# Attention and expert routing on one core: low parts on GpSimd, gating's count in spare columns of an output tile, rows stored in five pieces, a new order

## The chip, the core and the metric

One core of one Trainium2 chip. The metric is device time of one execution in microseconds; lower is better. The engines: PE is TensorE (matmuls; PEld its weight loads), DVE VectorE, ACT ScalarE, POOL GpSimd, SP SyncE, which here issues most of the DMAs. The clock of TensorE is granted by a throttle and can fall to half.

## The reference

```python
# q, k, v: (8 batches, 8 heads, 576, 64)
scores = scale * np.matmul(rotate(q), rotate(k).transpose(0, 1, 3, 2))   # rotate: rotary position
scores = scores - np.max(scores, axis=-1, keepdims=True)
attn = np.exp(scores)
attn = attn / (np.sum(attn, axis=-1, keepdims=True) + 1e-09)
x = np.matmul(attn, v)            # then to (4608 tokens, 512)
...
logits = x @ w_gate               # 8 experts
expert_idx = np.argmax(logits, axis=1)
gate_w = softmax(logits)[np.arange(N), expert_idx]
for e in range(8):
    mask = expert_idx == e
    out[mask] = gate_w[mask, None] * (np.maximum(x[mask] @ w1[e], 0) @ w2[e])   # 512 -> 1024 -> 512
```

## The kernel before

**Stages.** The first 610 us or so are attention, pair by pair: 8 batches of 4 pairs of heads (NP = 4), 32 pairs. Once a batch's four pairs are done, its rows are *gated*: logits (they come out of the matmul of O with the gate's weights beside the rows), maximum, softmax, one-hot of the chosen expert, a count (how many earlier rows chose the same expert) and a rank; the rows are stored to HBM (`x_dram`) and each row's number is written by an indirect DMA to its place in the expert's list (`xlist`). Then the experts' work runs over those lists, in slots of rows gathered by index; TensorE is busy through that stage, and the change does not touch it.

**Precision.** Scores are computed in two parts: a number is split into a high part (a copy rounded to fp32r) and a low part (the number less its high part), and three products high-high, low-high, high-low are summed.

**The order.** `PLAN` is a list of 67 tokens that `window(w)` goes through once for every w; a token ("S1p", 1) does step S1 of pair n = w - 1, and its last letter names the engine (p PE, v DVE, a ACT, g POOL, d a DMA issued on SP). So several pairs are in flight. Instructions of PE, DVE, ACT and POOL are chained in this order on their own engine. `GATE` places the steps of gating between the tokens: position `pos` means token pos % 67 of the window that lies pos // 67 after the last pair of the batch. `paced` makes a DMA wait for the last ACT instruction that was put into the order ahead of it.

**The steps of one pair.** FQ, FK load q and k (576 KB each: a copy and its rotated partner), VP loads v. RQ, RK rotate them: three 576-element operations on POOL each (`rotate`, L374 to L378), into one buffer `yq`, `yk` each. HQ, HK copy to the high part, LQ, LK subtract for the low part (L127 through `tt`, on DVE). DH, DL copy the halves of the high and of the low part to the other 64 partitions by DMA (`do_D`, L416, two DMAs each): the *moved halves*. cR gathers the last 64 columns into `zq` (L420); S4 uses that. S0 to S8 are score steps on PE (12 matmuls for S4 and 6 for each other one); M their row maximum (DVE, L444), E the exponential (ACT, L455). Scores lie in two PSUM banks of `ps_s`; O takes one of the same two. TA, TB, TR transpose; cA, cB, c1, c2, c3 copy the transposed weights to SBUF (L393). V0 to V9 multiply with v (L513); U copies the result; O transposes it back and adds the logits' columns (L534), X0 and X1 scale it into the batch's rows, ZD and RZ handle the row sums.

**Gating.** gL, gM, gD, gQ, gF, gB, gO, gV (DVE) lead from logits to the one-hot `oh`; gE, gG, gW give the weight; gP is the count on PE (`counted_`, matmuls at L645 and L647) in a bank of `ps_s` of its own; gR the rank from it (DVE); gU, gY the place; gS the store on SP (L624, L625: 1152 KB and 144 KB); gI0 to gI4 the indirect DMAs (L666, on POOL, paced). Inside the count:

```python
pc = bank()                                  # before: a tile of ps_s
nc.tensor.matmul(pc[:, 0:40], lhsT=upb, ...)
...
nc.tensor.matmul(pc[:, 64:72], lhsT=onesb, ...)
```

Of the kernel before, what the change touches and what calls it, by code (L numbers as in the profile page):

```python
# [7 lines left out]
F32 = mybir.dt.float32  # L8
# [26 lines left out]
]  # L35
GATE = [
    ("gLv", 246), ("gMv", 250), ("gDv", 250), ("gQv", 250), ("gFv", 250), ("gBv", 250), ("gOv", 250), ("gVv", 250),
    ("gEa", 252), ("gGv", 260), ("gWv", 260), ("gPp", 261), ("gSd", 265), ("gRv", 275), ("gUv", 283), ("gYv", 283),
    ("gI0g", 300), ("gI1g", 300), ("gI2g", 334), ("gI3g", 334), ("gI4g", 367),
]  # L40
W0 = -2
WARM = 80
RSTEP = (15, 17, 18, 45, 49, 50, 58)
WSPLIT = (24, 30, 47, 62)
NR = 2
CHAINED = ("EngineType.PE", "EngineType.DVE", "EngineType.Activation", "EngineType.Pool")


# [13 lines left out]
def kernel(  # L62
# [21 lines left out]
    cpool = ctx.enter_context(tc.tile_pool(name="cpool", bufs=1))  # L84
# [18 lines left out]
    x_dram = dpool.tile([NT, H * XW], F32, name="x_dram")  # L103
# [6 lines left out]
    V = nc.vector  # L110
    sm = ctx.enter_context(tc.tile_pool(name="sm", bufs=3))
# [14 lines left out]
    def tt(o, x, y, op):  # L126
        V.tensor_tensor(out=o, in0=x, in1=y, op=op)  # L127
# [270 lines left out]

    def do_LQ(st, n, eng):
        q = st["q"]  # L400
        tt(q[:, 0, 1], st["yq"], q[:, 0, 0].bitcast(F32), ALU.subtract)

    def do_HK(st, n, eng):
        st["k"] = rp.tile([P, 2, 2, HS], F32R, name="k2")
# [2 lines left out]
    def do_LK(st, n, eng):  # L407
        k = st["k"]
        hi, lo = (k[:, i].rearrange("p h s -> p (h s)") for i in range(2))
        tt(lo, st["yk"], hi.bitcast(F32), ALU.subtract)  # L410

    def do_D(st, n, part):

# [114 lines left out]
    def do_O(st, n):  # L528
# [24 lines left out]
    def do_X(st, n, h):  # L553
        b, pr = divmod(n, NP)
        nc.vector.tensor_tensor(
            out=batch(b)[:, :, 2 * pr + h, :], in0=st["O"][:, h, 0:5 * XW].rearrange("p (c w) -> p c w", w=XW),
            in1=st["rz"][:, :, h:h + 1].broadcast_to([P, 5, XW]), op=ALU.mult)

    def perform(tok, st, n):

# [19 lines left out]
        else:  # L580
            dict(RQ=do_RQ, RK=do_RK, ZD=do_ZD, RZ=do_RZ, O=do_O, TR=do_TR, cR=do_cR)[name](st, n)

    def gate(b, bank, spaced=True):

        batches.pop(b)
        xt = xt2[b % 2]
        L = sm.tile([P, 5, E], F32, name="L")
        mx = sm.tile([P, 5], F32, name="mx")
        dl = sm.tile([P, 5, E], F32, name="dl")
        ex, rk = gate_ex, gate_rk  # L590
        gs = sm.tile([P, 5], F32, name="gs")
# [16 lines left out]
        def at(eng):  # L608
            return nc.gpsimd if eng == "g" else V
# [10 lines left out]
        def weight(eng):  # L620
            V.reciprocal(out=xt[:, :, 0], in_=gs)

        def store(eng):
            nc.sync.dma_start(out=x_dram[b * S:b * S + 512, :].rearrange("(p i) d -> p i d", i=4), in_=xt[:, 0:4])  # L624
            nc.sync.dma_start(out=x_dram[b * S + 512:b * S + 576, :], in_=xt[0:64, 4])  # L625

        def equal(eng):
            tt(eq, L, mxb, ALU.is_equal)

        def scored(eng):  # L630
            at(eng).tensor_tensor(out=eq, in0=eq, in1=C("escore").unsqueeze(1).broadcast_to([P, 5, E]), op=ALU.mult)

        def best(eng):
            V.tensor_reduce(out=bs, in_=eq, axis=AX.X, op=ALU.max)

        def onehot(eng):
            tt(eq, eq, bs.unsqueeze(2).broadcast_to([P, 5, E]), ALU.is_equal)

        def masked(eng):
            at(eng).tensor_tensor(out=oh, in0=eq, in1=C("valid").unsqueeze(2).broadcast_to([P, 5, E]), op=ALU.mult)  # L640

        def counted_(eng):
            pc = bank()
            count.append(pc)
            nc.tensor.matmul(pc[:, 0:40], lhsT=upb, rhs=oh.rearrange("p c e -> p (c e)"), start=True, stop=False)  # L645
            for c in range(4):
                nc.tensor.matmul(pc[:, 8 * c + 8:40].rearrange("p (c e) -> p c e", e=E), lhsT=onesb,  # L647
                                 rhs=oh[:, c:c + 1, :].broadcast_to([P, 4 - c, E]), start=False, stop=(c == 3))
            for c in range(5):
                nc.tensor.matmul(pc[:, 64:72], lhsT=onesb, rhs=oh[:, c], start=(c == 0), stop=(c == 4))  # L650
# [13 lines left out]
        def listed(c):  # L664
            def f(eng):
                ins = nc.gpsimd.indirect_dma_start(  # L666
                    out=xlist, out_offset=bass.IndirectOffsetOnAxis(ap=lpi[:, c:c + 1], axis=0),
                    in_=tid[:, 5 * b + c:5 * b + c + 1], in_offset=None,
                    bounds_check=E * LCAP - 1, oob_is_err=False)
                tc.declare_no_dep(ins.ins, group="xlist", reason="the entries are disjoint")  # L670
                tc.add_to_no_dep_group("xlist", ins.ins)
                scattered.append(ins.ins)
                if spaced:
                    paced(ins)
            return f

        return dict(gL=logits, gM=top, gD=below, gE=exps, gG=total, gW=weight, gS=store, gQ=equal, gB=best,
                    gF=scored, gO=onehot, gV=masked, gP=counted_, gR=rank, gU=own, gY=place,
                    **{f"gI{c}": listed(c) for c in range(5)})

    def first_slots():
        assert len(scattered) == 5 * (B - 2)
# [37 lines left out]

    def gate_step(tok, b, ordered):
        if b not in gates:
            gates[b] = gate(b, lambda: ps_s.tile([P, 2, 512], F32, name="sp")[:, 0])
        chained_emit(lambda: gates[b][tok[:-1]](tok[-1]), ordered)

    def window(w, more={}, keep=lambda tok, n: True):
# [31 lines left out]
    def setup():  # L758

        nc.vector.tensor_copy(out=upb, in_=C("upper"))  # L760
        nc.vector.tensor_copy(out=tid, in_=C("tid"))
        nc.vector.tensor_copy(out=run, in_=C("ebase"))
        nc.vector.tensor_copy(out=gate_rk[:, :, E:E + 1], in_=C("bad").unsqueeze(2))
        for a, g in ((0, 0), (64, D)):
            r = slice(a, a + 64)
            nc.vector.tensor_copy(out=iw[r, :, E - g // 8:E - g // 8 + D], in_=ident[r, r].unsqueeze(1).broadcast_to([64, NP, D]))
            nc.sync.dma_start(out=iw[r, :, g:g + E], in_=w_gate.rearrange("(r p) e -> p r e", r=NP)[r])
        nc.sync.dma_start(out=xlist.rearrange("(p c) o -> p (c o)", p=P), in_=mark)
# [241 lines left out]
    reload(1, 2, regs1)  # L1010
    xtrans(1, 2)
    mm2(0, hs0, 2, False)
    last = gate(B - 1, lambda: ps_y.tile([P, DM], F32, name="yp"), False)
    for name, _ in GATE:
        last[name[:-1]](name[-1])
    slot(1, 2)
    route_rest()
    nc.gpsimd.memset(xsm, 0.0)
# [112 lines left out]
```

## Time and profile before

| | us |
|---|---|
| three runs, median (lowest to highest) | 1125.07 (1121.01 to 1126.71) |
| the profiled execution, its span | 1127.2, 1125.4 |
| TensorE busy in the span | 1027.6 (91%) |
| DVE, ACT, POOL busy | 737.2, 655.6, 417.6 |
| mean granted clock of TensorE | 0.940 of full speed |

A time at the head of a row is the start in the span; square brackets behind a row of the timeline hold how long the engine stood idle before it and on what, for example `<-DMA qk`. Rows of a group give the total busy time and the mean in ns of one. A share of the span averages stages: attention and the experts' stage have to be read apart, and attention window by window.

### The profile page before, as it was taken

The page shows a single profiled execution, that of the slowest core. Times are in us where ns is not written, and L with a number is a line of the kernel's source. Part 1 is how long each engine was busy: PE and PEld are TensorE (multiplying, and loading weights), DVE is VectorE, ACT ScalarE, POOL GpSimd, SP SyncE. Part 2 cuts the span into 40 slices and gives each one's busy share as a digit, 9 for nine tenths or more (in the row PEclk, how much of TensorE's full clock was granted, in tenths as well). Part 3 has the DMA queues.
Part 4 walks back from the last instruction along what each step waited for, and adds up shares of the span by engine and source line. Part 5 has one row for each costly group of instructions (what it writes and reads, how often), then busy time and mean ns, then how long its engine had stood idle before and what let it go on. Part 6 is the DMA issues. An engine that isn't in the chain of part 4 may idle for free. (4 is left out here: it accounts for less than half of the span.)

```text
span 1125.4 us, 25298 instructions
## 1 busy us (share of the span) xinstructions
PE 1027.6 (91%) x9720; PEld 812.9 (72%) x9720; DVE 737.2 (65%) x1188; ACT 655.6 (58%) x1180; POOL 417.6 (37%) x329
## 2 busy tenths in 40 slices
PE   4899889998898898798978989999999999999997
PEld 4666556666565565555656778999999999998886
DVE  6777757666567576575764565656666566665897
ACT  2787657666575575565667433545555445544886
POOL 5555365554554454645525231123112221112010
PEclk6799989989898899899998989999999999999999
DMA  7444674765746747556655041674262341124992
GB/s 237 129 132 132 140 126 138 135 119 153 97 126 132 103 131 143 106 164 107 119 170 118 15 88 33 198 251 153 67 190 59 123 148 50 42 65 151 355 350 91
DMA packets 91746, 151.47 MB, mean 135 GB/s; under 512 B 23207, under 2 KB 56231, under 8 KB 90592
## 3 DMA queue, kind: packets, MB, share of 16 engines
q1 hardware_dynamic: 83328, 127.66, 45.7%
q0 software_dynamic: 8000, 20.92, 6.0%
q8 instruction: 79, 1.29, 0.5%
q10 hardware_dynamic: 288, 1.18, 0.3%
q14 instruction: 51, 0.42, 0.1%
HBM read 162.47 MB, written 21.27 MB: 163 GB/s over the span
## 5 line engine op out<-in xcount | busy, mean ns | idle before, releaser
L444 DVE TENSOR_REDUCE negm<-sp 128x1 f32<-128x576 f32 x288 | 216.1, 754 | 173.4 <-PE sp L441 157.5
L455 ACT ACTIVATE pn<-sp,negm 128x576 f32<-128x576 f32 x256 | 189.8, 742 | 120.3 <-DVE negm L444 104.9
L441 PEld LDWEIGHTS sp<-k,q 64*128 64x128 f32 x1536 | 120.4, 200 | 97.9 <-issue 42.1
L441 PE MATMUL sp<-k,q 64*128 64x288 f32 x1536 | 180.2, 343 | 10.7 <-ACT pn L455 8.9
L513 PE MATMUL tp<-PT,vn 128*64 128x288 f32 x1024 | 172.2, 436 | 5.9 <-ACT PT L393 5.9
L896 PE MATMUL hp<-xh,w1h 128*128 128x256 f32 x544 | 155.5, 286 | 3.3 <-DVE hl L865 3.3
L896 PE MATMUL hp<-xl,w1h 128*128 128x256 f32 x544 | 155.2, 285 | 0.2 <-issue 0.2
L896 PE MATMUL hp<-xh,w1l 128*128 128x256 f32 x544 | 154.9, 285 | 0.0
L393 ACT COPY PT<-tp 128x1024 f32<-128x1024 f32 (+1 forms) x128 | 113.4, 905 | 45.2 <-PE tp L473 32.3
L835 DVE TENSOR_TENSOR w2l<-r,w2h 128x1024 fp32r<-128x1024 f32 x90 | 109.3, 1232 | 36.8 <-ACT w2h L834 34.4
L928 PE MATMUL yp<-w2h,hh 128*128 128x512 f32 x320 | 127.4, 398 | 0.0
L928 PE MATMUL yp<-w2l,hh 128*128 128x512 f32 x320 | 125.2, 391 | 0.0
L928 PE MATMUL yp<-w2h,hl 128*128 128x512 f32 x320 | 125.2, 391 | 0.0
L938 POOL DMA_INDIRECT out_dram<-y,gi x34 | 34.5, 1013 | 220.0 <-DVE y L131 196.2
L835 DVE TENSOR_TENSOR w1l<-r,w1h 128x1024 fp32r<-128x1024 f32 x92 | 109.3, 1229 | 4.3 <-ACT w1h L834 3.1
L896 PEld LDWEIGHTS hp<-xh,w1h 128*128 128x128 f32 x544 | 105.3, 194 | 5.6 <-DVE hl L865 3.6
L376 POOL TENSOR_TENSOR yq<-qk,rotq 128x576 f32<-128x576 f32 x31 | 44.7, 1442 | 168.3 <-DVE q L127 82.5
L896 PEld LDWEIGHTS hp<-xl,w1h 128*128 128x128 f32 x544 | 105.3, 194 | 0.9 <-issue 0.9
L896 PEld LDWEIGHTS hp<-xh,w1l 128*128 128x128 f32 x544 | 105.4, 194 | 0.8 <-issue 0.2
L473 PEld LDWEIGHTS tp<-cst,pn 64*128 64x128 f32 x2048 | 85.5, 154 | 19.8 <-ACT pn L455 8.8
L473 PE MATMUL tp<-cst,pn 64*128 64x64 f32 x2048 | 94.2, 242 | 4.4 <-issue 2.4
L864 ACT ACTIVATE hh<-hp 128x512 fp32r<-128x512 f32 x68 | 40.7, 598 | 96.7 <-PE hp L896 90.7
(201 smaller groups left out, 1818.7 us busy)
## 6 DMA issues: line engine op xcount, KB each, us to landing
r<-in_moe_w_dram SPq DMA_DIRECT2D x192, 512.0 KB
qk<-in_qk_dram SPq DMA_DIRECT2D x64, 576.0 KB
q<-q SPq DMA_DIRECT2D x128, 144.0 KB
x_dram<-xt SPq DMA_DIRECT2D x8, 1152.0 KB
vn<-in_v_dram SPq DMA_DIRECT2D x32, 256.0 KB
x_dram<-xt SPq DMA_DIRECT2D x8, 144.0 KB
vr<-in_v_dram SPq DMA_DIRECT2D x64, 16.0 KB
xlist<-tid,lpi POOLq DMA_INDIRECT x40
```

The source lines that it names most:

```text
L376: e.tensor_tensor(out=y, in0=x[0], in1=cos, op=ALU.mult)
L393: (nc.scalar.copy if eng == "a" else nc.vector.tensor_copy)(out=o, in_=i)
L441: nc.tensor.matmul(sp[:, u, 0:HS], lhsT=lhs, rhs=st["k"][r, kp, hc], start=(i_ == 0), stop=(i_ == len(todo) - 1))
L444: nc.vector.tensor_reduce(out=st["negm"][:, j:j + 1], in_=st["S", j][:, :, 0:HS], axis=AX.XY, op=ALU.max, negate=True)
L455: nc.scalar.activation(out=pt.rearrange("p (a b) -> p a b", a=2), in_=st.pop(("S", j))[:, :, 0:HS], func=AF.Exp, bias=st["negm"][:, j:j + ...
L473: nc.tensor.transpose(tp[:, b, c:c + 64], pn[r, i, k:k + P], ident[r, r])
L513: nc.tensor.matmul(st["av"][r, half, 0:HS], lhsT=st["vn"][:, h, kt, :] if kt < 4 else vr[n % NVR][:, r], rhs=st["PT"][:, h, kt, hs] if kt ...
L835: nc.vector.tensor_tensor(out=lo, in0=src, in1=hi.bitcast(F32), op=ALU.subtract)
L864: nc.scalar.activation(out=hh, in_=hp, func=AF.Relu)
L896: m = nc.tensor.matmul(hp[:, fi], lhsT=w[:, dc, fs], rhs=x[:, dc], start=(i == 0), stop=(i == len(prods) - 1))
L928: m = nc.tensor.matmul(yp[t], lhsT=h[:, fi, ts_], rhs=w[:, fi], start=(g == 0 and fi == 0 and i == 0), stop=(g == FQ - 1 and fi == 1 and i ...
L938: sc = nc.gpsimd.indirect_dma_start(out=out, out_offset=bass.IndirectOffsetOnAxis(ap=si[:, t:t + 1], axis=0), in_=y, in_offset=None, bound ...
```

## The change

- LQ and LK run on GpSimd in place of VectorE; HQ and HK on ScalarE in place of VectorE; U and c1 on VectorE in place of ScalarE.
- The order is new: all 67 tokens stand elsewhere, and the offsets are one less, so the windows begin one earlier (W0). The loads FK, FQ, VP stand at positions 27, 42 and 48 (before: 0, 37, 1); DL at 7 and DH at 61 (before 64 and 56); cR at 37 and S4 at 38; RK 2, LQ 3, LK 29, RQ 54 on POOL; S0 to S9 and V0 to V9 are grouped in another way.
- Gating's count gP is no longer a step of GATE. It is written in `do_O` of the first pair of the next batch (CP = 0), into columns 424 to 496 of O's own tile, and the rank gR is done right behind that pair's second X.
- The store has five pieces, gS0 to gS4 (four of 32 partitions, 288 KB each, and one of 144 KB), each paced and at a place of its own; the five indirect DMAs stand at (window 4: positions 3, 29, 54) and (window 5: positions 3 and 4); before, two at window 4 position 32, two at window 4 position 66, one at window 5 position 32.
- gF and gV are gone: equality and score are one operation, and a column of constants (`gate_eq`) keeps rows beyond the batch out of the one-hot.
- The last batch's gating does count and rank behind its gO.

```diff
 PLAN = [
-    ("FKd", -1), ("VPd", 0), ("E0a", 1), ("S1p", 1), ("V5p", 3), ("S3p", 1), ("c2a", 2), ("RZv", 3), ("M1v", 1),
-    ("E1a", 1), ("V6p", 3), ("M3v", 1), ("V7p", 3), ("S7p", 1), ("V8p", 3), ("HKv", 0), ("E3a", 1), ("M7v", 1),
-    ("LKv", 0), ("S8p", 1), ("V9p", 3), ("M8v", 1), ("c1a", 2), ("cRa", 0), ("E7a", 1), ("TA0p", 1), ("S4p", 0),
-    ("M4v", 0), ("Ua", 3), ("TA1p", 1), ("E8a", 1), ("Op", 3), ("RQg", -1), ("cA0a", 1), ("E4a", 0), ("TB1p", 1),
-    ("cA1v", 1), ("FQd", -2), ("cB1a", 1), ("TB0p", 1), ("S6p", 0), ("TRp", 1), ("c3v", 3), ("X1v", 3), ("X0v", 3),
-    ("M6v", 0), ("cB0a", 1), ("E6a", 0), ("S2p", 0), ("M2v", 0), ("HQv", -1), ("E2a", 0), ("V0p", 2), ("ZDd", 2),
-    ("V1p", 2), ("S5p", 0), ("DHd", -1), ("V2p", 2), ("LQv", -1), ("M5v", 0), ("S0p", 0), ("V3p", 2), ("E5a", 0),
-    ("V4p", 2), ("DLd", -1), ("M0v", 0), ("RKg", -1),
+    ("E0a", 0), ("c2a", 1), ("RKg", -1), ("LQg", -1), ("S2p", 0), ("V5p", 2), ("V6p", 2), ("DLd", -1), ("V7p", 2),
+    ("M2v", 0), ("E6a", 0), ("E2a", 0), ("RZv", 2), ("S5p", 0), ("S8p", 0), ("V8p", 2), ("V9p", 2), ("TA0p", 0),
+    ("HKa", -1), ("M5v", 0), ("E5a", 0), ("S7p", 0), ("M8v", 0), ("Uv", 2), ("TA1p", 0), ("E8a", 0), ("M7v", 0),
+    ("FKd", -2), ("cA0a", 0), ("LKg", -1), ("Op", 2), ("cA1v", 0), ("E7a", 0), ("TB0p", 0), ("TB1p", 0), ("X0v", 2),
+    ("X1v", 2), ("cRa", -1), ("S4p", -1), ("c3v", 2), ("cB0a", 0), ("cB1a", 0), ("FQd", -3), ("S3p", -1), ("TRp", 0),
+    ("V0p", 1), ("M4v", -1), ("V1p", 1), ("VPd", -2), ("M3v", -1), ("E4a", -1), ("S1p", -1), ("E3a", -1), ("M1v", -1),
+    ("RQg", -2), ("S0p", -1), ("V2p", 1), ("V3p", 1), ("HQa", -2), ("V4p", 1), ("E1a", -1), ("DHd", -2), ("ZDd", 0),
+    ("M0v", -1), ("c1v", 0), ("S6p", -1), ("M6v", -1),
 ]
 GATE = [
-    ("gLv", 246), ("gMv", 250), ("gDv", 250), ("gQv", 250), ("gFv", 250), ("gBv", 250), ("gOv", 250), ("gVv", 250),
-    ("gEa", 252), ("gGv", 260), ("gWv", 260), ("gPp", 261), ("gSd", 265), ("gRv", 275), ("gUv", 283), ("gYv", 283),
-    ("gI0g", 300), ("gI1g", 300), ("gI2g", 334), ("gI3g", 334), ("gI4g", 367),
+    ("gLv", 180), ("gMv", 210), ("gDv", 210), ("gQv", 210), ("gBv", 210), ("gOv", 210), ("gEa", 219), ("gGv", 223),
+    ("gWv", 223), ("gS0d", 228), ("gUv", 247), ("gYv", 247), ("gS1d", 249), ("gI0g", 271), ("gS2d", 295),
+    ("gI1g", 297), ("gS3d", 316), ("gI2g", 322), ("gI3g", 337), ("gI4g", 338), ("gS4d", 362),
 ]
-W0 = -2
+W0 = -3
...
+CP = 0
...
-        tt(q[:, 0, 1], st["yq"], q[:, 0, 0].bitcast(F32), ALU.subtract)
+        (nc.gpsimd if eng == "g" else nc.vector).tensor_tensor(out=q[:, 0, 1], in0=st["yq"], in1=q[:, 0, 0].bitcast(F32), op=ALU.subtract)
...
-        tt(lo, st["yk"], hi.bitcast(F32), ALU.subtract)
+        (nc.gpsimd if eng == "g" else nc.vector).tensor_tensor(out=lo, in0=st["yk"], in1=hi.bitcast(F32), op=ALU.subtract)
...
+        if n >= NP and n % NP == CP:
+            gates[n // NP - 1]["gP"](o[:, 0, 424:496])        # end of do_O
...
+        st["X"] = st.get("X", 0) + 1                           # end of do_X
+        if st["X"] == 2 and n >= NP and pr == CP:
+            gates[b - 1]["gR"]("v")
...
-        def store(eng):
-            nc.sync.dma_start(out=x_dram[b * S:b * S + 512, :].rearrange("(p i) d -> p i d", i=4), in_=xt[:, 0:4])
-            nc.sync.dma_start(out=x_dram[b * S + 512:b * S + 576, :], in_=xt[0:64, 4])
+        def store(g):
+            def f(eng):
+                if g < 4:
+                    r = slice(32 * g, 32 * g + 32)
+                    o, i = x_dram[b * S:b * S + 512, :].rearrange("(p i) d -> p i d", i=4)[r], xt[r, 0:4]
+                else:
+                    o, i = x_dram[b * S + 512:b * S + 576, :], xt[0:64, 4]
+                ins = nc.sync.dma_start(out=o, in_=i)
+                if spaced:
+                    paced(ins)
+            return f
...
-            tt(eq, L, mxb, ALU.is_equal)
-            at(eng).tensor_tensor(out=eq, in0=eq, in1=C("escore")..., op=ALU.mult)
+            V.scalar_tensor_tensor(out=eq[:, :, 0:E], in0=dl, scalar=0.0,
+                                   in1=C("escore")..., op0=ALU.is_equal, op1=ALU.mult)
...
-            pc = bank()
+        def counted_(pc):
             count.append(pc)
```

More of the change, by code (lines that the diff above doesn't have):

```diff
@@ L26 @@
 PLAN = [
[8 rows of a table removed]
[8 rows of a table added]
 ]
 GATE = [
-    ("gLv", 246), ("gMv", 250), ("gDv", 250), ("gQv", 250), ("gFv", 250), ("gBv", 250), ("gOv", 250), ("gVv", 250),
-    ("gEa", 252), ("gGv", 260), ("gWv", 260), ("gPp", 261), ("gSd", 265), ("gRv", 275), ("gUv", 283), ("gYv", 283),
-    ("gI0g", 300), ("gI1g", 300), ("gI2g", 334), ("gI3g", 334), ("gI4g", 367),
+    ("gLv", 180), ("gMv", 210), ("gDv", 210), ("gQv", 210), ("gBv", 210), ("gOv", 210), ("gEa", 219), ("gGv", 223),
+    ("gWv", 223), ("gS0d", 228), ("gUv", 247), ("gYv", 247), ("gS1d", 249), ("gI0g", 271), ("gS2d", 295),
+    ("gI1g", 297), ("gS3d", 316), ("gI2g", 322), ("gI3g", 337), ("gI4g", 338), ("gS4d", 362),
 ]
-W0 = -2
+W0 = -3
 WARM = 80
-RSTEP = (15, 17, 18, 45, 49, 50, 58)
-WSPLIT = (24, 30, 47, 62)
+RSTEP = (9, 12, 19, 22, 39, 46, 49)
+WSPLIT = (20, 25, 50, 60)
 NR = 2
+CP = 0
 CHAINED = ("EngineType.PE", "EngineType.DVE", "EngineType.Activation", "EngineType.Pool")
@@ L309 @@
     gate_rk = cpool.tile([P, 5, E + 1], F32, name="gate_rk")
+    gate_eq = cpool.tile([P, 5, E + 1], F32, name="gate_eq")
     lctx = ctx.enter_context(ExitStack())
@@ L581, in perform, with gate @@
             dict(RQ=do_RQ, RK=do_RK, ZD=do_ZD, RZ=do_RZ, O=do_O, TR=do_TR, cR=do_cR)[name](st, n)
-    def gate(b, bank, spaced=True):
+    def gate(b, spaced=True):
         batches.pop(b)
@@ L589, in gate @@
         dl = sm.tile([P, 5, E], F32, name="dl")
-        ex, rk = gate_ex, gate_rk
+        ex, rk, eq = gate_ex, gate_rk, gate_eq
         gs = sm.tile([P, 5], F32, name="gs")
-        eq = sm.tile([P, 5, E], F32, name="eq")
         bs = sm.tile([P, 5], F32, name="bs")
@@ L621, in weight @@
             V.reciprocal(out=xt[:, :, 0], in_=gs)
-        def store(eng):
-            nc.sync.dma_start(out=x_dram[b * S:b * S + 512, :].rearrange("(p i) d -> p i d", i=4), in_=xt[:, 0:4])
-            nc.sync.dma_start(out=x_dram[b * S + 512:b * S + 576, :], in_=xt[0:64, 4])
+        def store(g):
[9 more added lines that the diff above has]
+            return f
         def equal(eng):
-            tt(eq, L, mxb, ALU.is_equal)
-        def scored(eng):
-            at(eng).tensor_tensor(out=eq, in0=eq, in1=C("escore").unsqueeze(1).broadcast_to([P, 5, E]), op=ALU.mult)
+            V.scalar_tensor_tensor(out=eq[:, :, 0:E], in0=dl, scalar=0.0,
+                                   in1=C("escore").unsqueeze(1).broadcast_to([P, 5, E]), op0=ALU.is_equal, op1=ALU.mult)
         def best(eng):
@@ L636, in onehot @@
         def onehot(eng):
[L637 to L642, printed above, removed]
-            pc = bank()
+            tt(oh, eq[:, :, 0:E], bs.unsqueeze(2).broadcast_to([P, 5, E]), ALU.is_equal)
+        def counted_(pc):
             count.append(pc)
@@ L675, in listed @@
             return f
-        return dict(gL=logits, gM=top, gD=below, gE=exps, gG=total, gW=weight, gS=store, gQ=equal, gB=best,
-                    gF=scored, gO=onehot, gV=masked, gP=counted_, gR=rank, gU=own, gY=place,
-                    **{f"gI{c}": listed(c) for c in range(5)})
+        return dict(gL=logits, gM=top, gD=below, gE=exps, gG=total, gW=weight, gQ=equal, gB=best,
+                    gO=onehot, gP=counted_, gR=rank, gU=own, gY=place,
+                    **{f"gI{c}": listed(c) for c in range(5)}, **{f"gS{g}": store(g) for g in range(5)})
     def first_slots():
@@ L722, in gate_step @@
         if b not in gates:
-            gates[b] = gate(b, lambda: ps_s.tile([P, 2, 512], F32, name="sp")[:, 0])
+            gates[b] = gate(b)
         chained_emit(lambda: gates[b][tok[:-1]](tok[-1]), ordered)
@@ L762, in setup @@
         nc.vector.tensor_copy(out=run, in_=C("ebase"))
-        nc.vector.tensor_copy(out=gate_rk[:, :, E:E + 1], in_=C("bad").unsqueeze(2))
+        for t in (gate_rk, gate_eq):
+            nc.vector.tensor_copy(out=t[:, :, E:E + 1], in_=C("bad").unsqueeze(2))
         for a, g in ((0, 0), (64, D)):
@@ L1012 @@
     mm2(0, hs0, 2, False)
-    last = gate(B - 1, lambda: ps_y.tile([P, DM], F32, name="yp"), False)
+    last = gate(B - 1, False)
     for name, _ in GATE:
         last[name[:-1]](name[-1])
+        if name[:-1] == "gO":
+            last["gP"](ps_y.tile([P, DM], F32, name="yp"))
+            last["gR"]("v")
     slot(1, 2)
```

## The prediction

> **What bounds the kernel now.** I read the busy shares first, then stretches of the attention phase cut where the same token begins in successive windows, then the timeline around the stretches that are too long.
>
> ```profile
> span 1125.4 us, 25298 instructions
> PE 1027.6 (91%) x9720; PEld 812.9 (72%) x9720; DVE 737.2 (65%) x1188; ACT 655.6 (58%) x1180; POOL 417.6 (37%) x329
> ```
>
> The profiled run took 1127.2 us, 2.1 above the median of the three (1125.07). PE is the bound, but the share is an average. Stretches of the attention phase (columns: length, then busy time of PE, PEld, DVE, ACT, POOL, then granted clock, DMA share, GB/s):
>
> ```profile
> 319.36:334.78 15.42, 15.27 (x208) 10.24 (x208) 11.46 (x21) 11.97 (x25) 8.41 (x7) 1.00 0.49 137
> ```
> ```profile
> 61.36:107.65 46.29, 45.88 (x612) 30.78 (x612) 34.43 (x61) 35.96 (x75) 25.27 (x19) 1.00 0.50 136
> ...
> sum 549.04, PE 486.36 PEld 329.91 DVE 364.12 ACT 351.30 POOL 281.41; mean PE 60.80 PEld 41.24 DVE 45.52 ACT 43.91 POOL 35.18
> ```
> ```profile
> 107.65:127.20 19.55, 17.15 (x218) 11.35 (x217) 14.21 (x35) 12.10 (x26) 7.93 (x6) 0.91 0.58 175
> 127.20:147.74 20.54, 16.32 (x218) 10.84 (x216) 13.36 (x21) 11.84 (x25) 11.33 (x9) 0.99 0.75 93
> 147.74:167.94 20.20, 18.23 (x192) 12.81 (x194) 11.74 (x20) 12.04 (x27) 11.20 (x10) 0.84 0.65 113
> ...
> 295.71:319.36 23.65, 20.59 (x192) 14.03 (x194) 11.49 (x20) 12.00 (x27) 11.96 (x11) 0.71 0.60 92
> ```
>
> A window without gating takes 15.42 us with PE busy for 15.27 of it: nothing but TensorE's own instructions sets it. The eight stretches from 61.36 to 610.40 hold 29 windows (3, six times 4, 2) and sum to 549.04; 29 x 15.42 is 447.2. So 101.8 us are lost, and every loss lies next to gating: the first batch's three windows are 4.13, 5.12 and 4.78 too long, the worst window in the trace (295.71) 8.23. The MoE phase behind it has the same instructions after the change, so the forecast is about these 549 us.
>
> **Term A: gating's count.** Today it takes a score bank, and TensorE stands at it:
>
> ```profile
> PE sp L645 <- ACT pn L455: 16.0, 7, 2.5
> ```
> ```profile
> 118.68 0.18 PE L645 MATMUL sp<-oh,upb 128*128 128x40 bf16 x1 [2.27 <-ACT pn L455]
> 118.85 0.54 SPq L624 DMA_DIRECT2D x_dram<-xt  x1
> ```
> ```profile
> 119.90:123.30 3.40, 3.40 (x20) 1.77 (x16) 0.76 (x1) 1.01 (x3) 1.41 (x1) 0.50 1.03 367
> ```
>
> The wait columns are total us, times, longest: seven stalls, 16.0 us. One of 2.27 us is followed by 3.40 us at clock 0.50, in which half the work is lost, 1.7 us; together 4.0, and the window is 4.13 too long. In the new version the count goes to columns 424 to 496 of a tile that O has already got, after O's own matmuls, and its inputs come from steps 21 tokens (4.8 us of a 15.42 us window of 67) earlier. The wait goes in all seven batches: 7 x 4.13 = 28.9 (bounds 16.0, if the half clock comes from something else, and 28.9). What is late next: the rank now reads that tile, so S3, which takes the bank after O, waits for two more small DVE operations of about 0.2 us each (row of 199 ns below). S4 stands between O and S3 and covers that. DVE is busy 11.5 of 15.4.
>
> **Term B: the order on TensorE.**
>
> ```profile
> 325.12 1.19 PE L513 MATMUL tp<-PT,vn 128*64 128x288 f32 x8
> ...
> 326.24 0.67 PE L441 MATMUL sp<-k,q 64*128 64x288 f32 x6
> ...
> 326.84 0.71 PE L513 MATMUL tp<-PT,vn 128*64 128x288 f32 x4
> ...
> 327.48 0.66 PE L441 MATMUL sp<-k,q 64*128 64x288 f32 x6
> ...
> 335.11 1.05 PE L441 MATMUL sp<-k,zq 64*128 64x288 f32 x12
> ```
>
> A V step alone costs 0.64 us to the next start, two together 1.12, so each joint saves 0.16. An S step alone costs 0.60 to the next start; twelve S matmuls in a row take 1.05 instead of 1.20, 0.15 a joint. The old order has seven groups of V, the new one four (V5-V7, V8-V9, V0-V1, V2-V4): 0.48. The old one never puts two S steps together, the new one four times (S5 S8, S4 S3, S1 S0, S6 S2): 0.60. That is 1.08 us a window, 31 over 29 windows, if nothing else begins to wait. With two score banks, two S steps in a row also ask that two E steps be finished, so I take half, 0.5 x 29 = 14.5, between 0 and 31.
>
> **The other engines.** Time of one instruction (total and mean behind the bar):
>
> ```profile
> L127 DVE TENSOR_TENSOR k<-yk,k 128x576 fp32r<-128x576 f32 x32 | 28.5, 891 | 0.7 <-ACT k L393 0.7
> L127 DVE TENSOR_TENSOR q<-yq,q 128x576 fp32r<-128x576 f32 x32 | 24.3, 758 | 1.8 <-ACT q L393 0.7
> L393 DVE CAST q<-yq 128x576 fp32r<-128x576 f32 x31 | 17.0, 549 | 0.6
> ...
> L393 ACT CAST q<-yq 128x576 fp32r<-128x576 f32 x1 | 0.7, 671 | 5.8 <-DVE yq L378 5.8
> L393 DVE COPY PT<-tp 128x1024 f32<-128x1024 f32 x32 | 39.0, 1218 | 4.5 <-PE tp L473 4.2
> L393 ACT COPY uT<-tp 128x576 f32<-128x576 f32 x32 | 20.4, 637 | 8.5 <-PE tp L513 8.5
> L393 ACT COPY PT<-tp 128x512 f32<-128x512 f32 x32 | 18.5, 577 | 0.0
> L376 POOL TENSOR_TENSOR yq<-qk,rotq 128x576 f32<-128x576 f32 x31 | 44.7, 1442 | 168.3 <-DVE q L127 82.5 <-DMA qk<-in_qk_dram 67.7 <-DVE negm L444 12.2
> L666 POOL DMA_INDIRECT xlist<-tid,lpi x40 | 40.3, 1008 | 57.9 <-ACT pn L455 46.4 <-issue 6.9 <-PE tp L473 3.7
> L631 DVE TENSOR_TENSOR eq<-eq,cst 128x40 f32<-128x40 f32 x8 | 1.6, 199 | 0.2
> ```
>
> DVE loses LQ, LK, HQ and HK (0.758 + 0.891 + two of about 0.549) and gets U and c1 (by the 1024-element copy, 1218 x 576/1024 = 0.69 and 1218 x 512/1024 = 0.61): 11.46 - 2.75 + 1.30 = 10.0. ACT gets two casts of 0.671 for 0.637 + 0.577: 11.97 + 0.13 = 12.1. POOL gets two subtractions of the shape of the rotation's, 1.44 each: 8.41 + 2.88 = 11.3, with a scatter 12.3 of a window of 14.9. All are below PE, so no term. The Trainium skill (GPSIMD Engine Reference, 4.1 Engine selection) speaks against such a move: two-input elementwise work belongs on VectorE, GpSimd takes about twice as long. The rows agree (758 against 1442), but here POOL has the room; the sum is the same by both. Gating's DVE work falls by two operations of 0.199 us a batch. The store becomes five transfers: three more issues on SP of about 0.54 (row at 118.85), each behind the ACT work before it; SP has the room, but the moved halves and loads queue behind. They cost nothing as long as the loads have the room of the next part, and at worst a load waits one E step.
>
> **Term C: what scatters do to transfers.**
>
> ```profile
> 21.09 0.54 SPq L361 DMA_DIRECT2D qk<-in_qk_dram  x1
> ...
> 25.68 1.42 POOL L376 TENSOR_TENSOR yq<-qk,rotq 128x576 f32<-128x576 f32 x1 [4.34 <-DMA qk<-in_qk_dram]
> ```
> ```profile
> 128.87 1.15 POOL L666 DMA_INDIRECT xlist<-tid,lpi  x1 [7.50 <-ACT pn L455]
> ...
> 130.31 0.33 SPq L361 DMA_DIRECT2D qk<-in_qk_dram  x1
> 130.32 0.97 POOL L666 DMA_INDIRECT xlist<-tid,lpi  x1 [0.30 <-issue]
> ...
> 135.93 2.40 SPq L416 DMA_DIRECT2D q<-q  x4
> ...
> 142.50 1.42 POOL L376 TENSOR_TENSOR yq<-qk,rotq 128x576 f32<-128x576 f32 x1 [6.91 <-DMA qk<-in_qk_dram]
> ...
> 146.70 0.40 ACT L420 CAST zq<-q 128x256 fp32r<-128x256 f32 x1 [4.27 <-DMA q<-q]
> ...
> 147.89 1.81 PE L441 MATMUL sp<-k,zq 64*128 64x288 f32 x12 [3.44 <-ACT pn L455]
> ```
> ```profile
> ACT zq L420 <- DMA q<-q: 31.9, 9, 5.7
> POOL yq L376 <- DMA qk<-in_qk_dram: 54.6, 8, 9.3
> ```
>
> A load takes 4.6 us from issue to use (21.09 to 25.68). The one issued among a pair of scatters took 12.2, the moved halves issued at 135.93 let zq wait 4.27, and behind it TensorE stands 3.44 and then runs slow (0.84 over the window from 147.74). So a pair costs 7.6 us of transfer time, one scatter about 3.8. That is the rest of the loss: 101.8 - 28.9 = 73, or 10.4 a batch.
>
> The change lets three scatters stand alone and leaves gI3, gI4 as a pair. The load of k (FK) is issued at position 27, and HK needs its rotation at position 18 of the next window: 58 of 67 tokens, 13.3 us; less the rotation (three of 1.42) 9.0 us of room. Normal, 4.6, fits; one scatter, 8.4, just fits; the pair, 12.2, is 3.2 late, in all seven batches. To that 1.7 for a clock that halves as in term A, and about 3 for the moved halves issued five tokens behind gI3 (DL to cR has 30 tokens, 6.9 us): 8 a batch against 10.4, a gain of 17. Bounds: -73 (everything fits) and more than nothing lost, which is rival 3.
>
> **The sum.** 1127.2 - 28.9 - 14.5 - 17 = 1066.8, and 2.1 less against the median: **1065 us**. Start of the pipeline and the last gating (count and rank behind gO) I leave at nothing, within 3 us.
>
> **The rivals.**
>
> 1. *The stalls stay as large (1082).* If a scatter delays whatever is in flight whether it comes alone or in a pair, term C is 0: 1125.1 - 28.9 - 14.5 = 1082. For it: the moved halves, issued 5.6 us after the second scatter, were still late. Against it: the room of the loads grows. 0.25, with what lies from 1075 up to no change.
> 2. *All hidden (1009).* If a scatter alone delays little and the pair fits, the 101.8 go: 1125.1 - 101.8 - 14.5 = 1009. For it: in the quiet window POOL, ACT and DVE each idle 3 us or more. Against it: seven pairs remain. 0.18 for all below 1040.
> 3. *Slower (1182).* A late load now also holds LQ, because LQ stands behind RK on POOL's queue; LQ holds DL, that holds cR, and that S4 on TensorE. Before, LQ was on DVE and free of it. If scatters apart from each other make three such windows a batch, each as bad as the worst one (8.23): 7 x 24.7 = 173 in place of 73, 1125.1 - 28.9 - 14.5 + 100 = 1182. With two a batch, 115 in place of 73, it is 1124: two late windows of that size a batch decide the sign. For it: five scatters in four places instead of three, POOL at 12.3 of 14.9. Against it: only one of four places is a pair. The Trainium skill (DMA: Bandwidth & Descriptors, Queues, rings and completion order) has a rule on this side: a completion's semaphore write lands only after every earlier write of that DMA engine, in whatever queue. By it every one of the five scatters holds all that is in flight, and apart they hold more transfers than together; the late zq behind the scatters agrees. 0.11 slower, 0.06 about no change.
>
> **How the numbers follow.** 0.40 for the forecast, 1040 to 1075; 0.25, 0.18 and 0.17 for the rivals. 0.5% (5.6 us) is about what a measurement of this kernel can tell from no change. Faster 0.83, same 0.06, slower 0.11. The range, 1018 to 1118, leaves out the lower part of rival 2 (0.07) and most of rival 3 (0.13).
>
> **What would show it.** A: no wait of L645's successor for ACT and no clock of 0.50 behind O. B: quiet windows of about 14.9 (14.3 to 15.4). C: the pair gI3, gI4 followed by a late yk and HK once a batch, the other scatters by none; total waits for qk and for q<-q below 86 us. Wrong would be: quiet windows longer than 15.4 because E steps come too late for joined S steps; late zq behind single scatters; TensorE waiting on LQ through the moved halves.

## The result, and the profile after

Median 1071.8 us (1061.55 to 1074.72, 4 runs) against 1123.04 us before (four runs; the table of the kernel before has the first three): a ratio of 0.9524, 95% interval 0.9453 to 0.9596. The profiled execution took 1070.2 us.

The page's span and busy shares after the change:

```profile
span 1068.4 us, 25294 instructions
PE 979.7 (92%) x9720; PEld 804.5 (75%) x9720; DVE 702.9 (66%) x1113; ACT 651.9 (61%) x1178; POOL 503.4 (47%) x391
```

A window without gating, and the same 29 windows as before (columns as in the prediction: length, busy PE, PEld, DVE, ACT, POOL, clock, DMA share, GB/s), each from an answer for that stretch:

```profile
73.51:87.92 14.41, 14.41 (x206) 10.59 (x206) 10.46 (x18) 11.79 (x27) 11.17 (x9) 1.00 0.50 140
59.11:552.87 493.76, 443.95 (x5931) 324.04 (x5930) 332.38 (x630) 345.93 (x733) 346.56 (x259) 0.95 0.60 141
```

The quiet window fell from 15.42 to 14.41 us and TensorE is busy in all of it. 29 such windows are 417.9, so 75.9 us are lost beside gating, where it was 101.8. One batch, window by window:

```profile
102.32:117.38 15.06, 14.57 (x206) 10.57 (x206) 12.18 (x27) 12.07 (x28) 11.14 (x9) 1.00 0.53 139
117.38:133.49 16.11, 14.96 (x216) 10.91 (x216) 12.21 (x24) 11.96 (x27) 12.28 (x10) 1.00 0.60 166
```
```profile
133.49:152.11 18.62, 17.04 (x222) 12.16 (x222) 10.46 (x18) 12.31 (x27) 14.71 (x13) 0.91 0.81 117
152.11:173.59 21.48, 15.41 (x190) 11.32 (x190) 10.52 (x18) 11.27 (x25) 11.61 (x9) 0.84 0.51 129
```

The count now stands in the second of these windows (at 120.01), which is 1.70 us above a quiet one at a clock of 1.00; before, its window was 4.13 above. Most of the loss lies in the third window, in which four of the five scatters are issued, and in the fourth, right behind them. What is waited for between 60 and 600 us (total us, times, longest):

```profile
POOL yk L378 <- DMA qk<-in_qk_dram: 73.0, 28, 6.4
ACT zq L422 <- DMA q<-q: 32.3, 7, 6.5
PE sp L443 <- ACT zq L422: 26.9, 7, 5.6
```

Once a batch S4 stands for zq, and zq for the moved halves. No row of the count is among TensorE's waits. In the timeline of one such place:

```profile
215.75 1.01 POOL L675 DMA_INDIRECT xlist<-tid,lpi  x1 [0.16 <-issue]
216.78 1.43 POOL L403 TENSOR_TENSOR q<-yq,q 128x576 fp32r<-128x576 f32 x1
218.38 0.99 POOL L675 DMA_INDIRECT xlist<-tid,lpi  x1 [0.17 <-issue]
...
219.68 0.97 POOL L675 DMA_INDIRECT xlist<-tid,lpi  x1 [0.30 <-issue]
...
227.61 0.40 ACT L422 CAST zq<-q 128x256 fp32r<-128x256 f32 x1 [4.68 <-DMA q<-q]
...
228.06 1.81 PE L443 MATMUL sp<-k,zq 64*128 64x288 f32 x12 [4.00 <-ACT zq L422]
```

LQ is the L403 row: the low moved halves are issued right behind it, at the same moment as gI3 and gI4 and 2.5 us after gI2.

### The profile page after: what moved, and what is told of

Its sections match the earlier page's. It is cut to its first block, busy times and chain, and to the rows that moved or that the text cites. A ratio compares the mean times of both kernels' runs of the same rounds, so it can differ in the third digit from the quotient of the medians.

```text
span 1068.4 us, 25294 instructions
## 1 busy us (share of the span) xinstructions
PE 979.7 (92%) x9720; PEld 804.5 (75%) x9720; DVE 702.9 (66%) x1113; ACT 651.9 (61%) x1178; POOL 503.4 (47%) x391
## 4 chain that ended last, share of the span: by engine, by line
PE 59%; DMA 13%; issue 12%; DVE 6%; POOL 5%; ACT 4%; SPq 0%; POOLq 0%; another core or an unknown queue 0%; ACTq 0%; DVEq 0%
PE hp L906 15%; PE yp L938 14%; PE sp L443 11%; PE tp L515 10%; DMA q<-q 5%; PE tp L475 4%; DVE negm L446 3%; DMA qk<-in_qk_dram 3%; DMA out_dram<-y,gi 3%; ACT pn L457 3%; PE sp L536 2%; PE xps L861 1%; POOL xlist L675 1%; POOL q L403 1%; DMA xg<-x_dram,gi 1%
## 5 line engine op out<-in xcount | busy, mean ns | idle before, releaser
L446 DVE TENSOR_REDUCE negm<-sp 128x1 f32<-128x576 f32 x288 | 209.2, 753 | 164.8 <-PE sp L443 152.1
L443 PE MATMUL sp<-k,q 64*128 64x288 f32 x1536 | 160.4, 330 | 21.3 <-ACT pn L457 15.8
L443 PEld LDWEIGHTS sp<-k,q 64*128 64x128 f32 x1536 | 118.0, 198 | 73.5 <-ACT pn L457 43.5
L515 PE MATMUL tp<-PT,vn 128*64 128x288 f32 x1024 | 156.9, 426 | 1.7 <-ACT PT L395 1.7
L395 ACT COPY PT<-tp 128x1024 f32<-128x1024 f32 x96 | 94.3, 1014 | 20.7 <-PE tp L475 16.1
L515 PEld LDWEIGHTS tp<-PT,vn 128*64 128x64 f32 x1024 | 63.8, 138 | 46.8 <-issue 16.8
L844 ACT CAST w2h<-r 128x1024 fp32r<-128x1024 f32 x90 | 92.7, 1043 | 5.1 <-PE yp L938 2.7
L475 PE MATMUL tp<-cst,pn 64*128 64x64 f32 x2048 | 88.5, 229 | 6.0 <-ACT pn L457 1.9
```

The costliest lines, as they stand in the source:

```text
L395: (nc.scalar.copy if eng == "a" else nc.vector.tensor_copy)(out=o, in_=i)
L443: nc.tensor.matmul(sp[:, u, 0:HS], lhsT=lhs, rhs=st["k"][r, kp, hc], start=(i_ == 0), stop=(i_ == len(todo) - 1))
L446: nc.vector.tensor_reduce(out=st["negm"][:, j:j + 1], in_=st["S", j][:, :, 0:HS], axis=AX.XY, op=ALU.max, negate=True)
L475: nc.tensor.transpose(tp[:, b, c:c + 64], pn[r, i, k:k + P], ident[r, r])
L515: nc.tensor.matmul(st["av"][r, half, 0:HS], lhsT=st["vn"][:, h, kt, :] if kt < 4 else vr[n % NVR][:, r], rhs=st["PT"][:, h, kt, hs] if kt ...
L844: nc.scalar.copy(out=hi, in_=src)
```

## The experiments

Times are medians; the ratio is to the kernel before, run beside it. The kernel before had medians from 1118.9 to 1126.6 us in these groups of runs, so a few us between kernels of different groups tell nothing. "Lost" is always the 29 windows less 29 quiet ones of the same kernel (75.9 in the changed kernel, 101.8 before), from its one profiled execution.

**The count alone, in the old order (e3), and the later scatters alone (e9).**

```diff
 # e3 and e9, on the kernel before: gU and gY 35 tokens later, the scatters a window (67 tokens) later
-("gUv", 283), ("gYv", 283), ("gI0g", 300), ("gI1g", 300), ("gI2g", 334), ("gI3g", 334), ("gI4g", 367)
+("gUv", 318), ("gYv", 318), ("gI0g", 367), ("gI1g", 367), ("gI2g", 401), ("gI3g", 401), ("gI4g", 434)
 # e3 only: count in do_O, rank behind the second X, as in the change
+            gates[n // NP - 1]["gP"](o[:, 0, 424:496])
```

> The kernel before with one part of the change: count in the spare columns behind O of the next batch's first pair, rank behind its second X; what follows the rank is a window later (scatters at the same positions of the window). Old order, old engines, one store. Theory A: the seven waits at L645 and the half clock behind them go, 1123 - 28.9 = 1094 (16 at least: 1107). Rival (TensorE waits as long at the next score step, because S waits for the rank): within 4 us of 1123.

> The kernel before with only the place of what follows the rank moved as in e3_old_order_spare: place at window 4 position 50 and the scatters one window later, at the same positions of it. The count stays in a score bank. e3 gained 49 us where the bank wait was priced at 28.9. Theory S (20 of the 49 come from the scatters' being away from the window that the count stalls): 1123 - 20 = 1103. Rival A+ (all 49 hang on the count's stall, whose half clock and lateness also make the scatters' stalls): 1123 within 5 us.

e3: 1074.32 us, ratio 0.9565 (0.9496 to 0.9635). e9: 1091.58 us, 0.972 (0.9667 to 0.9773). The 29 windows of e3, then of e9:

```profile
61.49:559.69 498.20, 461.27 (x5932) 308.76 (x5932) 363.87 (x699) 350.18 (x736) 276.09 (x203) 0.98 0.59 144
```
```profile
61.65:568.60 506.95, 466.41 (x5932) 310.28 (x5932) 358.33 (x699) 350.14 (x735) 275.23 (x203) 0.96 0.56 142
```

e3, with the old order, old engines and one store, comes within 2.5 us of the whole change. Two thirds of that are not the count: moving the scatters one window later gives 34 us by median, and the count another 17. The split is not sharp: the 29 windows of the two profiled executions differ by 8.75 us only. What the count's move does is seen in the window that holds it in e9, and in the same window and the next one of e3:

```profile
107.97:127.54 19.57, 17.18 (x218) 11.36 (x218) 13.89 (x33) 12.09 (x27) 7.92 (x6) 0.91 0.56 175
```
```profile
107.79:124.41 16.62, 15.35 (x208) 10.23 (x206) 13.52 (x31) 12.09 (x27) 7.94 (x6) 1.00 0.55 158
124.41:140.43 16.02, 15.81 (x218) 10.61 (x216) 12.24 (x25) 11.89 (x26) 8.84 (x7) 1.00 0.62 182
```
```profile
118.81 0.66 PE L441 MATMUL sp<-k,q 64*128 64x288 f32 x6 [1.14 <-ACT pn L455]
```

Without the stall the window is 2.95 us shorter and its clock is 1.00 instead of 0.91: here the slow clock went with the stall. But TensorE now waits 1.14 us for an exponential in the same window of e3 (the last row), and the next window, which holds the count there, is 0.62 above its neighbour in e9 (15.40). That leaves 2.3 us in this batch, where the prediction had 4.13; seven times that would be 16, in place of 28.9. In e9 the waits at the count are as before, but POOL stands at a scatter for an exponential once, for 6.1 us; waits between 60 and 600 us:

```profile
PE sp L645 <- ACT pn L455: 16.0, 7, 2.5
...
ACT zq L420 <- DMA q<-q: 11.6, 8, 2.4
...
POOL xlist L666 <- ACT pn L455: 6.1, 1, 6.1
```

In the kernel before, POOL's scatters waited 46.4 us for ACT, and zq 31.9 (both rows stand in the prediction). A scatter that waits on POOL's queue for a step of ACT holds the rotation behind it, and with it everything up to zq. That is one way in which the old place was bad; which part of the 34 us is this wait and which the transfers, these two runs don't separate.

**The bank again, in the new order (e2).**

```diff
-            gates[n // NP - 1]["gP"](o[:, 0, 424:496])
+            gates[n // NP - 1]["gP"](ps_s.tile([P, 2, 512], F32, name="sp")[:, 0])
```

> The changed kernel with the count in a score bank of its own again, at the same place behind O. Theory A (the bank wait and the half clock behind it cost 4 us a batch): TensorE waits for ACT's exponential at the count or at the next score step for 1.5 to 3 us in each of seven batches, the first window of a batch grows from 15.06 to 17 to 19, total 1072 + 14 to 28, so 1086 to 1100. Rival (the old order made that wait, in the new one the bank is free in time): within 4 us of 1072.

1077.65 us, 0.9614 (0.954 to 0.9689), which overlaps with the changed kernel's interval. The count finds its bank free, right behind O, here and at the other batches (no wait for an exponential before it):

```profile
119.15 1.28 PE L536 MATMUL sp<-iw,uT 64*128 64x72 f32 x20
120.59 0.18 PE L654 MATMUL sp<-oh,upb 128*128 128x40 bf16 x1
```

The rival holds: at the new place the count does not stall with or without spare columns. What it is worth there is between nothing and some 6 us.

**The joints (e4) and the engines (e7).**

```diff
 # e4: two V steps between S steps again
-("DLd", -1), ("V7p", 2), ... ("S5p", 0), ("S8p", 0) ... ("S0p", -1), ("V2p", 1)
+("DLd", -1), ... ("S5p", 0), ("V7p", 2), ("S8p", 0) ... ("V2p", 1), ("S0p", -1)
 # e7: LQv, LKv, HKv, HQv, Ua, c1a in the new order
```

> The changed kernel with four joints on TensorE undone: V7 goes between S5 and S8, V2 between S1 and S0. Theory B (each joint saves 0.15 or 0.16 us because TensorE alone sets the quiet window): quiet windows 14.40 + 0.62 = 15.0, total 1072 + 18 = 1090. Rival (quiet windows became shorter because of the other engines, HQ, HK, LQ, LK, U, c1 elsewhere): quiet windows stay within 0.15 of 14.40, total within 4 us of 1072.

> The changed kernel with the engines of before in the new order: LQ, LK, HQ, HK on DVE, U and c1 on ACT. Theory B (the quiet window is TensorE's own instructions, so who does the small work does not matter there): quiet windows 14.4 to 14.6. For the lost time, Theory L (LQ behind RK and the scatters on POOL's queue is what makes DL late): lost time falls from 76 to about 50, total 1045. Rival (DL is late because of the transfers themselves, not LQ): lost time stays at 70 to 80, total within 5 us of 1072; DVE, which gets 1.4 us more a window, may cost another 10.

e4: 1081.83 us, 0.9638 (0.957 to 0.9706). e7: 1128.4 us, 1.0052 (1.0014 to 1.009). The quiet window of e4, then one of e7:

```profile
75.67:90.82 15.15, 15.08 (x206) 10.41 (x206) 10.72 (x19) 12.11 (x26) 11.13 (x9) 1.00 0.49 138
```
```profile
78.36:94.26 15.90, 14.88 (x208) 10.75 (x206) 12.23 (x20) 11.74 (x27) 8.43 (x7) 1.00 0.48 132
```

Four joints cost 0.74 us a window (0.62 expected): the quiet window is TensorE's own instructions. That gives 21 us over 29 windows, but the 29 windows grew by 11.4 only (505.17 against 493.76; the total by 10 by median), since the lost time fell from 75.9 to 65.8. A slower window may give the transfers more room; that is not shown. e7's total went the way neither theory said. With DVE doing the low and high parts (12.23 us busy) the new order no longer fills TensorE (14.88 of 15.90), and its waits between 60 and 600 us are for ACT's exponentials:

```profile
PE sp L443 <- ACT pn L457: 50.0, 58, 2.6
...
PE sp L443 <- ACT zq L422: 12.2, 7, 3.3
```

The likely reading: grouped S steps ask for their banks sooner, and only with the moved work do the maxima and exponentials follow. e7 takes six steps back at once, so which of them matters is not shown. The order and the engines are one change, not two; the new order on the old engines is no faster than no change. S4's wait for zq is smaller there (12.2 against 26.9), but the lost time is not: its 29 windows take 541.41 us, 80 more than 29 of 15.90. So theory L (LQ on POOL makes the loss) fell, as far as the total lost goes.

**No scatters (e5), one store (e8).**

```diff
 # e5: gI0 to gI4 taken out of GATE (the lists stay empty)
 # e8: store at the place of gS0, unpaced, as before; gS1 to gS4 taken out
```

> The changed kernel without its forty indirect DMAs to xlist (the experts' lists stay empty, so the rows of the result are not written; the attention stage is what is read). Theory C (all that gating still costs beyond its own instructions, 76.2 us in 29 windows, comes from those scatters): lost time in 29 windows falls from 76.2 to below 20, every window between 14.4 and 15.6, TensorE's wait for zq gone. Rival (the five pieces of the store do it, 10 transfers a batch beside the loads): at least 40 us stay lost, windows over 18 us remain.

> The changed kernel with the store of before in place of its five pieces: one of 1152 KB and one of 144 KB at the place of the first piece, not paced. Theory P (five pieces put a transfer of 288 KB between the loads in five places, among them beside the scatters): lost time falls from 76 to 60 or less, total 1055 or less. Rival P- (one store of 1152 KB fills the DMA engines for 3.4 us and more and delays the loads behind it, which the pieces avoid): the window of the store grows by 2 to 4 us, total 1072 + 14 to 28. If neither: within 5 us of 1072, and the pieces are worth nothing.

e5, a single run, of which only the attention phase is read: 1009.75 us. e8: 1084.68 us, 0.9679 (0.9629 to 0.9729). The 29 windows of e5, then of e8:

```profile
59.19:499.59 440.40, 426.58 (x5932) 312.45 (x5930) 331.57 (x631) 344.35 (x732) 315.28 (x228) 0.99 0.55 156
```
```profile
60.19:565.82 505.63, 449.00 (x5932) 327.73 (x5930) 328.01 (x630) 345.74 (x732) 347.54 (x261) 0.94 0.61 138
```

The third and fourth window of the first batch in e5, 18.62 and 21.48 us in the changed kernel:

```profile
133.50:147.89 14.39, 14.39 (x206) 10.59 (x206) 10.45 (x19) 11.73 (x26) 11.14 (x9) 1.00 0.63 183
147.89:162.28 14.39, 14.39 (x206) 10.57 (x206) 10.46 (x19) 11.79 (x27) 11.16 (x9) 1.00 0.53 149
```

Without scatters both are quiet windows. 22.5 us stay lost (440.40 - 417.9), in the windows of gating's own instructions and at the end of attention; zq is in no wait of that run. So the scatters cost 53.4 us, 7.6 a batch. Theory C is right in the main, though it forecast less than 20 lost and the second window is 16.08 us even here. The DMA columns point at the transfers: in the third window the DMA engines are busy for 0.81 of the time and move 117 GB/s, without scatters 0.63 and 183. A scatter is 512 bytes; what costs is that the transfers beside it take longer for their bytes.

One store in place of the five paced pieces, which the prediction had at nothing, costs about 12 us: the 29 windows take 505.63 against 493.76. The pieces are not a load beside the scatters but a relief: S4's wait for zq was 44.4 us in ten places with one store. That is near rival P-, not theory P. Whether the size, the places or the pacing does it was not tried.

**Where the scatters stand (e1, e6, e10, e12, e13).**

```diff
 # changed kernel: gI0 (window 4, position 3)  gI1 (4, 29)  gI2 (4, 54)  gI3 (5, 2)  gI4 (5, 3)
 # e1_spread:          (4, 18)   (4, 52)   (5, 18)   (5, 52)   (6, 18)
 # e6_pair_behind:     as before, but gI3 (5, 12), gI4 (5, 13)
 # e10_pair_after_LK:  as before, but gI3 (5, 29), gI4 (5, 30)
 # e12_late_scatter:   (5, 3)    (5, 29)   (5, 54)   (6, 3)    (6, 4)
 # e13_all_after_LK:   (4, 29)   (4, 30)   (5, 29)   (5, 30)   (6, 29)
```

In `GATE` gI3 and gI4 stand at 337 and 338, so at positions 2 and 3 of window 5, one less than in the list of the change and in some of the expectations below.

> The five scatters alone and away from the moved halves: window 4 positions 18 and 52, window 5 positions 18 and 52, window 6 position 18. Theory D (the loss is the low moved halves, issued at position 7 among scatters, which land only with them: zq and with it S4 are late by 5 us): no wait of zq for q<-q above 1 us, the fourth window of each batch falls from about 22 to below 16 us, 30 to 45 us faster than the changed kernel's 1072, so 1027 to 1042. Rival F (the load of k behind the pair is late, as the prediction had it): the pair is gone too, so 5 us a batch, about 1040; it cannot be told from D by this run. Rival N (a scatter costs the same wherever it stands): the loss of 2 to 7 us moves to other windows, total within 5 us of 1072.

> The changed kernel with its pair of scatters gI3, gI4 at positions 12 and 13 in place of 3 and 4: still a pair, but issued behind the low moved halves (DL, position 7). Theory D (the loss is DL, which lands only with scatters issued around it): zq waits under 1 us behind the pair, the fourth window of a batch goes from about 22 to below 17 us, total 1072 - 35 = 1037. Rival F, the prediction's own mechanism (the load of k, issued at 27 behind the pair, comes too late for HK): the pair still holds that load, the stall stays or grows, 1072 or more.

> The changed kernel with the pair gI3, gI4 behind LK (positions 29, 30 in place of 3, 4), some 4 us later than DL is issued (at 12, 13 the pair had moved by 0.1 us only, since POOL came late there). Theory D (DL lands only with scatters issued around it): zq no longer waits in the fourth window, 22 to below 18 us; what the pair holds then is the load of k at 27, needed 9 us later; total 1072 - 20 to 35, so 1037 to 1052. Rival F (the load of k behind a pair is late): zq's wait moves one window on, as large as before, total within 6 us of 1072.

> The changed kernel with all five scatters one window later, at the same positions: what e9 did to the old order, where 34 us went. Theory S (scatters hurt when they run beside the pieces of the store, which stand at windows 3, 4 and 5; a window later only the last piece is left): lost time falls from 76 to 50, total about 1045. Rival (in the new order the loss is the scatters' place against DL and the load of k, which the shift leaves as it is): within 6 us of 1072.

> The changed kernel with every scatter behind LK, so none is issued in the 4 us around DL: gI0, gI1 at window 4 positions 29, 30, gI2, gI3 at window 5 positions 29, 30, gI4 at window 6 position 29. In e10 (1060) the wait of zq that is left follows gI2, issued at 147.21 just ahead of LQ at 148.25. Theory D (what counts is a scatter in flight when DL is issued): zq waits under 1 us in all batches, lost time in 29 windows from 64 to 40 or less, total 1035 or less. Rival F (two pairs now hold two loads of k a batch, and HK comes late): lost time stays at 60 to 80, waits of POOL for qk above 80 us, total 1055 to 1075.

| | median us | ratio to before (interval) | lost in 29 windows |
|---|---|---|---|
| e1 | 1106.26 | 0.986 (0.9778 to 0.9943) | 113 |
| e6 | 1073.25 | 0.9525 (0.9489 to 0.956) | 80 |
| e10 | 1059.96 | 0.9462 (0.941 to 0.9513) | 64 |
| e12 | 1078.14 | 0.9614 (0.9569 to 0.966) | 82 |
| e13 | 1069.2 | 0.9569 (0.9447 to 0.969) | 70 |

Theory D's forecasts of 1027 to 1052 us (e1, e6, e10) and of 1035 or less (e13) came true in none, nor did theory S's 1045 for e12, whose rival (within 6 us of 1072) is nearly met. e6 told nothing: POOL came late to those places, so the pair moved by 0.1 us only. e10, where it moved by 5 to 6 us, has the best median of all kernels here, though its interval overlaps with that of the changed kernel. There the fourth window of one batch lost its wait for the moved halves, while another kept it. First the one that lost it, then the other, each with gI2 ahead of LQ (L403) and the pair:

```profile
214.91 1.01 POOL L675 DMA_INDIRECT xlist<-tid,lpi  x1 [0.15 <-issue]
...
215.95 1.42 POOL L403 TENSOR_TENSOR q<-yq,q 128x576 fp32r<-128x576 f32 x1
...
223.08 0.40 ACT L422 CAST zq<-q 128x256 fp32r<-128x256 f32 x1 [2.58 <-POOL yq L380]
...
223.10 1.01 POOL L675 DMA_INDIRECT xlist<-tid,lpi  x1 [0.15 <-issue]
```
```profile
147.21 1.01 POOL L675 DMA_INDIRECT xlist<-tid,lpi  x1 [0.15 <-DMA x_dram<-xt]
148.25 1.44 POOL L403 TENSOR_TENSOR q<-yq,q 128x576 fp32r<-128x576 f32 x1
...
155.39 1.01 POOL L675 DMA_INDIRECT xlist<-tid,lpi  x1 [0.15 <-issue]
...
159.77 0.41 ACT L422 CAST zq<-q 128x256 fp32r<-128x256 f32 x1 [6.64 <-DMA q<-q]
```

e13's expectation blames gI2, issued 1 us ahead of LQ, for the wait that stayed. But gI2 stands 1 us ahead of LQ in both batches; what differs in these rows is the pair, issued behind zq's cast in the first and ahead of it in the second. e13 took gI2 away from there, the waits stayed, and theory D in its narrow form (only a scatter within some 4 us of DL hurts) fell. Moved halves issued from 142 on lie between one pair and the next, and the cast that needs them comes late:

```profile
139.08 1.14 POOL L675 DMA_INDIRECT xlist<-tid,lpi  x1 [0.16 <-ACT PT L395]
...
140.53 0.98 POOL L675 DMA_INDIRECT xlist<-tid,lpi  x1 [0.30 <-issue]
142.26 6.07 SPq L418 DMA_DIRECT2D q<-q  x4
...
155.63 1.01 POOL L675 DMA_INDIRECT xlist<-tid,lpi  x1 [0.15 <-issue]
...
164.24 0.40 ACT L422 CAST zq<-q 128x256 fp32r<-128x256 f32 x1 [12.55 <-DMA q<-q]
```

A scatter is long. The issues of e10, then of e13 (the last number is the median time to landing, of the few scatters whose landing the profile tells: three of 40 in e10, from 7.5 to 11.5 us, and six in e13, from 8.0 to 11.2):

```profile
xlist<-tid,lpi POOLq DMA_INDIRECT x40, 8.3
```
```profile
xlist<-tid,lpi POOLq DMA_INDIRECT x40, 9.4
```

My reading: with a window of 14.4 us, two of 8 to 9 us cover most of it, so moving a scatter mostly chooses which transfer lies beside it. e12's loss moved with its scatters (the fourth window's to the one behind it) and stayed as large; in e1, spread widest, S4's wait grew to 35.9 us. No theory of these runs holds for all of them: rival N (the same cost wherever a scatter stands) forecast 1072 within 5 us for e1, and it was 34 above. Rival F's total for e13 (1055 to 1075) came true, its sign did not: POOL's waits for qk were 48.7 us, not above 80. That scatters can be placed at 64 and at 113 us lost is shown; a rule that gives the number is not. Why the old order with one store loses 51 (e3) where the new one loses 76 was not tried apart from e4, whose slower windows lost 66. The intervals of e6, e10, e13 and the changed kernel overlap, so which of these places is best is not shown.

## Why the prediction was right, point by point

- **The total.** 1065 against 1071.8, inside the range. But it is a sum of terms off in both directions, and that they nearly cancel is luck: of the 55.3 us between 549.04 and 493.76, the quiet windows gave 29 (14.5 predicted), the lost time 26 (28.9 + 17 predicted). Of these 26, one store would take away about 12 (e8) and a bank for the count nothing to 6 (e2); the rest is not told apart.
- **Term A** was mis-sized. The step that failed: seven times the 4.13 us by which the count's window was too long, as if nothing came in the stall's place. In the old order the stall and the slow clock behind it both go, but a wait of 1.14 us comes back in the same window and the count takes 0.62 in the next (e9 to e3). By medians the move is worth 17 us. That is next to the lower bound of 16.0 by chance, since that bound assumed that the half clock would stay. In the new order there is no stall even with a bank (e2).
- **Term B** came out whole. The two stated rows gave 1.08 us a window, measured 1.01; halving it for engines that might not follow was the wrong choice, because the same change moves work so that they can. e7 shows that the worry itself was right: without the moved work the window is 15.90.
- **Other engines.** DVE 10.46, ACT 11.79 and POOL 11.17 in the quiet window, against 10.0, 12.1 and 11.3 worked out.
- **Term C** had the scatters' share nearly right by luck, and its mechanism wrong. 8 us a batch were expected to remain and 7.6 are the scatters' (e5). But TensorE waits for the moved halves of q (26.9 us at S4), not for a late HK, and the prediction took the remainder for the whole loss: 22.5 us without any scatter stay on top, and so 76 remained instead of 56. Its own sign said so: the waits for qk and for q<-q were to fall below 86 us and were 105 (73.0 and 32.3). Rival 1, stalls as large as before, has this term right: 73 by its sum.
- **The store** was costed at nothing; its paced pieces save about 12 us (e8).
- **Rival 3** (late loads holding LQ, DL and cR) names the right chain with the wrong size: once a batch, 7 us, not three times 8.2. e1 went its way with 1106, short of its 1124 to 1182. The rule of the Trainium skill (DMA: Bandwidth & Descriptors, Queues, rings and completion order) that a completion waits for every earlier write of its DMA engine fits e10 and e13, where moved halves land late behind scatters on another queue. It spoke against spreading, and e1 agrees: 113 us lost where the changed kernel loses 76. No run separates this rule from transfers that are merely slower beside a scatter.

## What to carry to other kernels

Read the quiet window and the disturbed ones apart, and price a change in each: here joining steps on TensorE paid in full in the quiet window, 1.0 us of 15.4, but only with the small work moved to other engines (e7). A stall's price is not all that its window is too long: here stall and slow clock went, something else waited in their place, and 17 us came of the 28.9 that had been counted. Before moving small scattered writes about, measure how long one is in flight; here it was more than half the period, and most places traded one late transfer for another. With no scatters at all 53 us went; fewer of them, or work that does not wait for a transfer, were not tried.

## What the runs showed of the hardware

An indirect DMA of 128 four-byte rows to HBM took 7.5 to 11.5 us to land beside this traffic, medians 8.3 (e10) and 9.4 (e13) where the profile tells it. Beside scatters, in the third window of a batch, the DMA engines moved 117 GB/s at a busy share of 0.81; without them (e5) it was 183 at 0.63. A cast that needed transfers issued on another queue among scatters waited 12.55 us for them (e13). The prediction's 3.8 us for one was the delay of a load, not the landing. A two-input operation of 576 columns on GpSimd took 1.42 us, no longer than the 1.44 of the rotation's before, though VectorE was busy for 10.46 of 14.41 us.
